# Linear attention with one routed expert on one core: tile 0's k evicted in one piece, tile 3's root on GpSimd, G of tile 0 after q unit 1

## The chip, the core and the metric

The kernel runs on one core of a Trainium2 chip. The metric is the device time of one execution in microseconds; the number to compare is the median of several. The core's engines each follow an instruction list of their own, in order, and wait for each other by semaphores: TensorE (PE in the profile), VectorE (DVE), ScalarE (ACT), GpSimd (POOL), and SyncE (SP), which here only issues DMAs.

## What is computed

One block over 2048 tokens of width 640, in bf16. With `xn` the layer norm of `x`, the output is `x + xn`, plus linear attention on `xn`, plus a small gated network that is applied to the 8 tokens with the largest router value and added to those rows.

```python
def _A_ref(x, wqkv, wo):                 # called with xn
    q, k, v = qkv[0], qkv[1], qkv[2]     # 32 heads of 20
    phi = lambda t: jnp.where(t > 0, t + 1, jnp.exp(t)) + 1e-6
    pq, pk = phi(q), phi(k)
    kv = jnp.einsum("bhsd,bhse->bhde", pk, v)
    z = jnp.einsum("bhsd->bhd", pk)
    num = jnp.einsum("bhqd,bhde->bhqe", pq, kv)
    den = jnp.einsum("bhqd,bhd->bhq", pq, z)[..., None] + 1e-6
    o = num / den
    return (lambda x, *d: x.transpose(*d))(o, 0, 2, 1, 3).reshape(B, S, D) @ wo
...
xn = _layernorm(x, axis=-1)
return x + _A_ref(xn, A_wqkv, A_wo) + _B_ref(xn, B_w_r, B_w_gate, B_w_up, B_w_down)
```

`_B_ref` (the routed network) returns its input `xn` with the 8 updated rows, which is where the `xn` in the sum comes from.

## The kernel before

The 2048 tokens are 16 tiles of 128 rows. The kernel sets the order of the instructions by hand: what the program emits first for an engine, that engine runs first. The places in the code of the functions named here are printed below.

For a tile t the first stage does this:

- `stat(t, 0)` and `stat(t, 1)` on VectorE (L176, L178): the mean and variance of the 640 columns, in two halves and an aggregate, into `mv`.
- The root: one over the square root of the variance, into `rs`. `root_act` does it on ScalarE as exp(-0.5 ln(v + eps)) in two instructions (L182, L183); `root_pool` does it on GpSimd as an addition and a power (L187, L188). Before the change tiles 0 to 3 and 8 are done by ScalarE, the others by GpSimd.
- `norm_dve(t)` on VectorE (L197) writes the normalized tile `xn`.
- The tile is transposed into `xnT`, columns on the partitions. For tiles 0 to 3 TensorE does it (`tr_pe`, L216) into PSUM banks 7 and 6, and `tr_ev` copies three of the five blocks out on ScalarE (L222) and two on VectorE (L227). For tiles 4 to 15 it is a transposing DMA that SP issues (`tr_dma`, L230).
- `k_half(t, 0)` and `k_half(t, 1)` (L238): k of the tile by TensorE, 320 columns each, from the stationary tile of `xnT`. The halves go to PSUM banks 2 and 3 for tile 1, 4 and 5 for tile 2, and 0 and 1 for the others.
- `k_act(t)` on ScalarE (L255, L256): an exp and a relu from PSUM for each half, into `ek` and `rk`, and for tiles from 1 on a copy of the router's column (L258). `k_phi(t)` on VectorE (L262) joins them into `pk`, the feature map of k.
- `g1(t)` (L269): five matmuls that add the tile's share of G = xn^T pk (first 512 columns) into banks 2 to 6.

Between these, `q_mm(u)` (L277) computes one of 20 units of q, 128 columns by 512 tokens, transposed, into bank 7 (unit 1 into bank 0); `q_act` (L286, L287) and `q_phi` (L293) apply the feature map as for k.

`const_sel8` (L368 to L375) builds a small constant mask on GpSimd, a memset and four selections; it is first used long after, in the routed network.

SP's list in this stretch: the loads of x up to tile 9 and of the q weights, then `tr_dma(4)`, `tr_dma(5)`, `tr_dma(6)`, `load_x(10, 16)` (one load of the last six tiles, 960 KB, L99), `tr_dma(7)`, and then a transpose and a weight load in turn.

From `for t in range(5, T)` (L483) on, a loop runs the same steps for the later tiles, with the normalization four tiles ahead of k. Then come the attention's small matrix products, the routed network, the remaining units of q, and the output tiles (L833 and after).

The change touches the order of calls between L410 and L460.

Of the kernel before, what the change touches and what calls it, by code (L numbers as in the profile page):

```python
# [38 lines left out]
def kernel(  # L39
# [26 lines left out]
    def sb(name, shape, dtype=BF16):  # L66
        return sm.tile(shape, dtype, tag=name, name=name)
# [30 lines left out]
    def load_x(a, b):  # L98
        SP.dma_start(x_sb[:, a:b, :], x_v[:, a:b, :])  # L99
# [52 lines left out]
    def router_col():  # L152
        PE.transpose(psb[:, 6, 512 : 512 + KC], wr5[:], ident[0:KC, 0:KC])
        A.copy(wk[:, :, D], psb[:, 6, 512 : 512 + KC])

    def router_0():
        for kc in range(KC):
            PE.matmul(
                ps[:, 6, 400:401], lhsT=xnT[:, kc, 0:P], rhs=wk[:, kc, D : D + 1],
                start=(kc == 0), stop=(kc == KC - 1),  # L160
            )
# [13 lines left out]
    def stat(t, b):  # L175
        V.bn_stats(out=stats[:, t, b, :], in_=x_sb[:, t, b * HW : (b + 1) * HW])  # L176
        if b:
            V.bn_aggr(out=mv[:, t, :], in_=stats[:, t, :, :])  # L178

    def root_act(t):  # L180
        sl = slice(t, t + 1)
        A.activation(lg[:, sl], mv[:, t, 1:2], AF.Ln, bias=eps5[:])  # L182
        A.activation(rs[:, sl], lg[:, sl], AF.Exp, scale=-0.5)  # L183

    def root_pool(t, n=1):
        sl = slice(t, t + n)
        G.tensor_scalar_add(t2[:, sl], mv[:, sl, 1], EPS_BF16)  # L187
        G.tensor_tensor(out=rs[:, sl], in0=t2[:, sl], in1=mhalf[:, 0:n], op=ALU.pow)  # L188
# [7 lines left out]
    def norm_dve(t):  # L196
        V.tensor_scalar(  # L197
            out=xn[:, t, :], in0=x_sb[:, t, :], scalar1=mv[:, t, 0:1], scalar2=rs[:, t : t + 1],
            op0=ALU.subtract, op1=ALU.mult,
        )  # L200
# [19 lines left out]
    def tr_ev(t, other=A):  # L220
        dst = xnT[:, :, t * P : (t + 1) * P]
        A.copy(dst[:, 0:3, :], psb[:, 7, 0 : 3 * P].rearrange("p (k f) -> p k f", k=3))  # L222
        src = psb[:, 6, 0 : 2 * P].rearrange("p (k f) -> p k f", k=2)
        if other is A:
            A.copy(dst[:, 3:, :], src)
        else:
            V.tensor_copy(dst[:, 3:, :], src)  # L227

    def tr_dma(t):
        nc.sync.dma_start_transpose(xnT[:, :, t * P : (t + 1) * P], xn[:, t, :])  # L230
# [3 lines left out]
    def k_half(t, b):  # L234
        b0 = K_BANK.get(t, 0)
        n = HW + (b if t else 0)
        for kc in range(KC):
            PE.matmul(  # L238
                ps[:, b0 + b, 0:n],
                lhsT=xnT[:, kc, t * P : (t + 1) * P],  # L240
                rhs=wk[:, kc, b * HW : b * HW + n],
                start=(kc == 0), stop=(kc == KC - 1),
            )
# [3 lines left out]
    def k_act(t, halves=(0, 1)):  # L247
        b0 = K_BANK.get(t, 0)
        if t not in kev:
            e = evk.tile([P, 2, HW], BF16, tag="ek", name=f"ek{t}")  # L250
            r = evk.tile([P, 2, HW], BF16, tag="rk", name=f"rk{t}")
            kev[t] = e, r
        e, r = kev[t]
        for b in halves:
            A.activation(e[:, b, :], ps[:, b0 + b, 0:HW], AF.Exp)  # L255
            A.activation(r[:, b, :], ps[:, b0 + b, 0:HW], AF.Relu)  # L256
            if b and t:
                A.copy(r_all[:, t : t + 1], ps[:, b0 + 1, HW : HW + 1])  # L258
# [8 lines left out]
    def g1(t):  # L267
        for c in range(5):
            PE.matmul(  # L269
                ps[:, 2 + c, :], lhsT=xn[:, t, c * P : (c + 1) * P], rhs=pk[:, t, 0:512],  # L270
                start=(t == 0), stop=(t == T - 1),
            )

    def q_mm(u, bank=7):
        tb, m = u // KC, u % KC
        for kc in range(KC):
            PE.matmul(  # L277
                ps[:, bank, :], lhsT=wq[:, kc, m * P : (m + 1) * P],
                rhs=xnT[:, kc, tb * 512 : (tb + 1) * 512],
                start=(kc == 0), stop=(kc == KC - 1),  # L280
            )

    def q_act(u, bank=7):
        e = evq.tile([P, 512], BF16, tag="eq", name=f"eq{u}")
        r = evq.tile([P, 512], BF16, tag="rq", name=f"rq{u}")
        A.activation(e[:], ps[:, bank, :], AF.Exp)  # L286
        A.activation(r[:], ps[:, bank, :], AF.Relu)  # L287
        kev["q", u] = e, r
# [79 lines left out]
    def const_sel8():  # L368
        cst["sel8"] = sb("sel8", [P, C], F32)
        G.memset(cst["sel8"][:], 0.0)  # L370
        for j in range(4):
            G.affine_select(
                out=cst["sel8"][:], in_=cst["sel8"][:], compare_op=ALU.not_equal, fill=1.0,
                base=-32 * j, pattern=[[-1, C]], channel_multiplier=1,
            )  # L375
# [9 lines left out]
    def stats2(t):  # L385
        stat(t, 0)
        stat(t, 1)
# [22 lines left out]
    tr_ev(1, V)  # L410
    root_act(2)
    router_col()
    k_act(0, (0,))
    stat(3, 0)
    norm_dve(2)
    stat(3, 1)
    const_sel8()
    k_half(1, 0)
    tr_pe(2)
    k_half(1, 1)  # L420
    tr_ev(2, V)
    root_act(3)
    k_act(0, (1,))
    router_0()
    k_act(1)
    stat(4, 0)
# [21 lines left out]
    norm_dve(5)  # L448
    tr_dma(5)
    q_act(0)  # L450
    g1(0)
    q_mm(1, 0)
    q_act(1, 0)
    k_phi(1)
    norm_dve(6)
    tr_dma(6)
    load_x(10, 16)
    stats2(7)
    root_pool(7)
    k_phi(2)  # L460
# [475 lines left out]
```

## Time and profile before

| | |
|---|---|
| median of 3 runs | 111.95 us (111.92 to 112.37) |
| the profiled execution | 112.4 us |
| its span, first to last instruction | 110.7 us |
| TensorE, matmuls | busy 105.0 us, 95% |
| VectorE | busy 83.2 us, 75% |
| ScalarE | busy 62.0 us, 56% |
| GpSimd | busy 41.0 us, 37% |
| granted TensorE clock | 1.0 in every slice |

In the rows below, a timeline row has the start in us, the length in us, the engine, the line of the kernel, the operation, the tile it writes and those it reads, the shapes and the count of instructions merged into the row; in brackets stands how long the engine was idle ahead of it and what ended that. Lengths of neighbouring instructions of one engine overlap a little, since an instruction begins while the one before it drains. A row of the chain of waits has the start, the length and what the end of the program was waiting for at that time. A row of the stretch table has the stretch, its length, and for matmuls, weight loads, VectorE, ScalarE and GpSimd the busy time with the count in brackets, then the granted clock, the busy share of the DMA engines and GB/s. SPq is SP issuing a DMA; the row of a DMA queue has packets, MB, and the share of 16 engines' time in the window.

### The profile page before, as it was taken

What the parts mean: (1) busy time and instruction counts of PE and PEld (TensorE: products, weight loads), DVE (VectorE), ACT (ScalarE), POOL (GpSimd) and SP (SyncE); (2) the same over time, 40 slices, a digit from 0 to 9 for tenths busy, and PEclk for the clock granted to TensorE, in tenths of its full rate; (3) what the DMA queues carried; (4) which work ended last, traced back from release to release, by engine and by line L of the source; (5) the groups of instructions that cost most, each with busy time, mean ns of one, the idle gap of its engine ahead of it and who ended that gap; (6) DMA issues with size and microseconds to landing.
All of it is one profiled execution on the core that took longest, in us unless ns stands there. A gap on an engine that the chain in (4) does not pass through costs nothing.

```text
span 110.7 us, 2559 instructions
## 1 busy us (share of the span) xinstructions
PE 105.0 (95%) x926; PEld 61.4 (55%) x926; DVE 83.2 (75%) x186; ACT 62.0 (56%) x160; POOL 41.0 (37%) x88
## 2 busy tenths in 40 slices
PE   5989799999999999999999999999999999999990
PEld 2256454665555565554436879534447766666660
DVE  1789987877999998753919964698599664788880
ACT  1449996799776666665019445588985735000000
POOL 6930273120067755899999430000000410000310
PEclk9999999999999999999999999999999999999999
DMA  3999237791758799989999979729928195783333
GB/s 84 325 341 331 103 65 63 131 328 20 197 138 160 194 182 220 199 189 287 259 248 401 391 260 266 219 68 319 356 79 177 32 330 188 169 322 118 114 121 118
DMA packets 28551, 22.46 MB, mean 203 GB/s; under 512 B 11634, under 2 KB 27258, under 8 KB 28538
## 3 DMA queue, kind: packets, MB, share of 16 engines
q1 hardware_dynamic: 23664, 18.44, 60.8%
q10 hardware_dynamic: 4810, 3.85, 11.1%
q8 instruction: 7, 0.11, 0.5%
q14 instruction: 6, 0.05, 0.2%
q0 software_dynamic: 64, 0.01, 0.1%
HBM read 14.79 MB, written 5.43 MB: 183 GB/s over the span
## 4 chain that ended last, share of the span: by engine, by line
PE 54%; DVE 22%; DMA 11%; POOL 5%; ACT 3%; issue 2%; SPq 0%; POOLq 0%; ACTq 0%
PE ps L833 19%; PE ps L277 12%; DMA x_sb<-in_A_x_dram 8%; DVE pk L262 6%; DVE stats L176 5%; DVE xn L197 5%; PE ps L269 5%; PE ps L531 4%; DVE pqT L293 3%; DMA xnT<-xn 3%; PE ps L238 3%; POOL rs L188 2%; DVE mv L178 2%; PE ps L685 2%; PE ps L768 2%
## 5 line engine op out<-in xcount | busy, mean ns | idle before, releaser
L238 PE MATMUL ps<-wk,xnT 128*128 128x320 bf16 (+1 forms) x160 | 25.0, 300 | 1.1 <-ACT xnT L222 1.0
L277 PE MATMUL ps<-xnT,wq 128*128 128x512 bf16 x100 | 23.7, 379 | 0.0
L833 PE MATMUL ps<-late,pqT 128*128 128x320 bf16 x150 | 21.8, 300 | 0.1
L238 PEld LDWEIGHTS <-xnT 128*128 128x128 bf16 x160 | 15.1, 97 | 9.7 <-ACT xnT L222 1.6
L269 PE MATMUL ps<-pk,xn 128*128 128x512 bf16 x80 | 19.6, 379 | 0.0
L255 ACT ACTIVATE ek<-ps 128x320 bf16<-128x320 f32 x32 | 14.6, 457 | 8.4 <-PE ps L238 8.4
L833 PEld LDWEIGHTS <-pqT 128*128 128x128 bf16 x150 | 13.9, 98 | 7.2 <-DVE pqT L640 1.9
L176 DVE BATCH_NORM_STATS2 stats<-x_sb 128x6 f32<-128x320 bf16 x32 | 14.7, 474 | 3.3 <-DMA x_sb<-in_A_x_dram 3.3
L286 ACT ACTIVATE eq<-ps 128x512 bf16<-128x512 f32 x20 | 12.0, 598 | 8.9 <-PE ps L277 8.9
L293 DVE SCALAR_TENSOR_TENSOR pqT<-eq,rq 128x512 bf16<-128x512 bf16 x20 | 14.2, 710 | 3.3 <-ACT rq L287 3.1
L842 DVE TENSOR_TENSOR o<-ps,x_sb 128x640 bf16<-128x640 f32 x15 | 12.4, 824 | 5.4 <-PE ps L833 3.0
L262 DVE SCALAR_TENSOR_TENSOR pk<-ek,rk 128x640 bf16<-128x640 bf16 x16 | 13.1, 823 | 3.2 <-ACT rk L256 3.2
L277 PEld LDWEIGHTS <-wq 128*128 128x128 bf16 x100 | 9.4, 98 | 10.6 <-issue 0.7
L256 ACT ACTIVATE rk<-ps 128x320 bf16<-128x320 f32 x32 | 14.6, 457 | 0.0
L208 POOL TENSOR_SCALAR x_sb<-x_sb,rs,nm 128x640 bf16<-128x640 bf16 x13 | 13.9, 1079 | 0.6
L269 PEld LDWEIGHTS <-xn 128*128 128x128 bf16 x80 | 7.6, 98 | 8.1
L287 ACT ACTIVATE rq<-ps 128x512 bf16<-128x512 f32 x20 | 11.9, 593 | 0.0
L187 POOL TENSOR_SCALAR t<-mv 128x1 bf16<-128x1 f32 x11 | 3.6, 326 | 22.2 <-DVE mv L178 22.0
L197 DVE TENSOR_SCALAR xn<-x_sb,mv,rs 128x640 bf16<-128x640 bf16 x16 | 8.3, 516 | 3.1 <-POOL rs L188 2.4
L188 POOL TENSOR_TENSOR rs<-t,mhalf 128x1 f32<-128x1 bf16 x11 | 9.4, 858 | 0.9
L884 POOL DMA_INDIRECT s_dram<-y,idx_i x1 | 1.6, 1594 | 20.4 <-ACT y L880 20.4
L869 ACT CAST o<-ps 128x160 bf16<-128x160 f32 x1 | 0.3, 293 | 13.9 <-PE ps L859 13.9
(129 smaller groups left out, 104.2 us busy)
## 6 DMA issues: line engine op xcount, KB each, us to landing
wg<-in_B_w_gate_dram SPq DMA_DIRECT2D x5, 384.0 KB, 3.4
wu<-in_B_w_up_dram SPq DMA_DIRECT2D x5, 384.0 KB, 8.9
wd<-in_B_w_down_dram SPq DMA_DIRECT2D x4, 480.0 KB, 11.0
spare<-rd SPq DMA_DIRECT2D x3, 640.0 KB, 5.5
rd<-rden ACTq DMA_DIRECT2D x1, 1280.0 KB, 7.1
out_dram<-o SPq DMA_DIRECT2D x8, 160.0 KB, 2.3
out_dram<-o ACTq DMA_DIRECT2D x7, 160.0 KB, 2.6
wo<-in_A_wo_dram SPq DMA_DIRECT2D x2, 500.0 KB, 8.2
```

Source lines behind the costliest of these rows:

```text
L176: V.bn_stats(out=stats[:, t, b, :], in_=x_sb[:, t, b * HW : (b + 1) * HW])
L197: V.tensor_scalar(out=xn[:, t, :], in0=x_sb[:, t, :], scalar1=mv[:, t, 0:1], scalar2=rs[:, t : t + 1], op0=ALU.subtract, op1=ALU.mult,)
L208: G.tensor_scalar(out=x_sb[:, t, :], in0=x_sb[:, t, :], scalar1=rs1[:, sl], scalar2=nm[:, sl], op0=ALU.mult, op1=ALU.add,)
L238: PE.matmul(ps[:, b0 + b, 0:n], lhsT=xnT[:, kc, t * P : (t + 1) * P], rhs=wk[:, kc, b * HW : b * HW + n], start=(kc == 0), stop=(kc == KC ...
L255: A.activation(e[:, b, :], ps[:, b0 + b, 0:HW], AF.Exp)
L256: A.activation(r[:, b, :], ps[:, b0 + b, 0:HW], AF.Relu)
L262: V.scalar_tensor_tensor(out=pk[:, t, :].rearrange("p (b f) -> p b f", b=2), in0=e[:], scalar=1.0, in1=r[:], op0=ALU.min, op1=ALU.add,)
L269: PE.matmul(ps[:, 2 + c, :], lhsT=xn[:, t, c * P : (c + 1) * P], rhs=pk[:, t, 0:512], start=(t == 0), stop=(t == T - 1),)
L277: PE.matmul(ps[:, bank, :], lhsT=wq[:, kc, m * P : (m + 1) * P], rhs=xnT[:, kc, tb * 512 : (tb + 1) * 512], start=(kc == 0), stop=(kc == K ...
L293: V.scalar_tensor_tensor(out=pqT[:, m, tb * 512 : (tb + 1) * 512], in0=e[:], scalar=1.0, in1=r[:], op0=ALU.min, op1=ALU.add,)
L833: PE.matmul(ps[:, b0 + b, 0:HW], lhsT=pqT[:, kc, t * P : (t + 1) * P], rhs=Ms[:, kc, b * HW : (b + 1) * HW], start=(kc == 0), stop=(kc == ...
L842: V.tensor_tensor(out=o_t[:], in0=ps[:, b0 : b0 + 2, 0:HW], in1=x_sb[:, t, :].rearrange("p (b f) -> p b f", b=2), op=ALU.add,)
```

## The change

```diff
@@ -410,17 +410,16 @@
     tr_ev(1, V)
     root_act(2)
     router_col()
-    k_act(0, (0,))
+    k_act(0)
     stat(3, 0)
     norm_dve(2)
     stat(3, 1)
+    root_pool(3)
     const_sel8()
     k_half(1, 0)
     tr_pe(2)
     k_half(1, 1)
     tr_ev(2, V)
-    root_act(3)
-    k_act(0, (1,))
     router_0()
     k_act(1)
     stat(4, 0)
@@ -448,13 +447,13 @@
     norm_dve(5)
     tr_dma(5)
     q_act(0)
-    g1(0)
     q_mm(1, 0)
     q_act(1, 0)
     k_phi(1)
     norm_dve(6)
     tr_dma(6)
     load_x(10, 16)
+    g1(0)
     stats2(7)
     root_pool(7)
     k_phi(2)
```

ScalarE evicts both halves of tile 0's k ahead of its copy of tile 2's transposed blocks, where the second half came after that copy and after tile 3's root. Tile 3's root goes from ScalarE to GpSimd, where it stands ahead of `const_sel8`; after `const_sel8` comes tile 4's root, as before. On TensorE the five matmuls of `g1(0)` come after those of q unit 1 instead of ahead of them. The amount of arithmetic is the same, and the weights of the later key-value product stay 128 columns wide.

## The prediction

> **What bounds the kernel now.** I read the chain of waits first. T4 to T15 below are the transposing DMAs of tiles 4 to 15 (`tr_dma`, L230), written by SP.
>
> ```profile
> span 110.7 us, 2559 instructions
> ...
> 19.43 6.15 DMA x_sb<-in_A_x_dram
> ...
> 47.02 3.30 DMA xnT<-xn
> ...
> 50.37 1.54 PE ps L238 x10
> ```
>
> Two stretches set the end. From 19.43 to 50.33 it is load_x(10, 16), then VectorE, then T15. From 50.37 it is TensorE alone, as the stretch table and TensorE's own timeline show:
>
> ```profile
> 50.37:107.71 57.34, 57.26 (x645) 35.14 (x645) 42.15 (x86) 26.12 (x52) 15.63 (x23) 1.00 0.74 227
> ...
> 13.14 1.54 PE L238 MATMUL ps<-wk,xnT 128*128 128x320 bf16 x10 [0.78 <-ACT xnT L222]
> ...
> 50.37 1.54 PE L238 MATMUL ps<-wk,xnT 128*128 128x320 bf16 x10 [0.16 <-DMA xnT<-xn]
> ```
>
> TensorE is busy for 57.26 of the last 57.34 us. Ahead of that it waits 0.78 us for ScalarE at 13.14 (tile 3's transposed half, L222), and 0.16 us for T15 at 50.37. The two limits almost meet: a TensorE that starts its dense part sooner gains at most 0.16 us unless T15 lands sooner, and a later T15 costs its full delay. So the change is judged by when load_x(10, 16) is issued.
>
> VectorE's first wait after 18 us that matters, and SP's issues ahead of the load:
>
> ```profile
> 25.60 0.49 DVE L176 BATCH_NORM_STATS2 stats<-x_sb 128x6 f32<-128x320 bf16 x1 [1.45 <-DMA x_sb<-in_A_x_dram]
> ...
> 15.63 2.43 SPq L230 DMA_TRANSPOSE xnT<-xn  x1
> ...
> 18.15 1.23 SPq L230 DMA_TRANSPOSE xnT<-xn  x1
> 19.43 0.57 SPq L99 DMA_DIRECT2D x_sb<-in_A_x_dram  x1
> ...
> L230 SPq DMA_TRANSPOSE xnT<-xn x12: 1202/1208/2431, 13.5 to 47.0; - x12
> ```
>
> VectorE stands idle for 1.45 us until the load lands. The load's issue follows T6 by 1.28 us (18.15 to 19.43); T6 follows T5, whose issue took 2.43 us where the median of the twelve is 1.21. Had T5 taken 1.21, SP would have been free at 16.84, and T6 would have waited for its own tile instead.
>
> **The change, part by part.** First ScalarE between 9.2 and 13 us:
>
> ```profile
> 9.22 0.44 ACT L256 ACTIVATE rk<-ps 128x320 bf16<-128x320 f32 x1
> 9.78 0.48 ACT L222 COPY xnT<-ps 128x384 bf16<-128x384 bf16 x1
> 10.16 0.30 ACT L182 ACTIVATE lg<-mv,eps 128x1 f32<-128x1 f32 x1
> 10.49 0.20 ACT L183 ACTIVATE rs<-lg 128x1 f32<-128x1 f32 x1
> 10.60 0.42 ACT L255 ACTIVATE ek<-ps 128x320 bf16<-128x320 f32 x1
> ...
> 11.23 0.44 ACT L255 ACTIVATE ek<-ps 128x320 bf16<-128x320 f32 x1
> ...
> 12.54 0.55 ACT L222 COPY xnT<-ps 128x384 bf16<-128x384 bf16 x1
> ```
>
> Tile 0's second half of k (10.60 to 11.23, two instructions, 0.63 us from start to start) moves ahead of tile 2's copy and starts about 9.55, as ScalarE issues such an instruction every 0.32 us. Tile 2's copy then starts at 10.20 instead of 9.78 (0.42 later). Tile 3's root (10.16 to 10.60, 0.44) goes away, and so does the wait of about 0.2 ahead of 9.78. The copy of tile 3 can therefore start at 10.20 + 0.38 (a copy's step, 9.78 to 10.16) + 1.31 (k of tile 1, 11.23 to 12.54) = 11.89 instead of 12.54, if TensorE has transposed tile 3 by then.
>
> Next the root of tile 3 on GpSimd. Rows of the nearest one, tile 4's, with VectorE around it, and tile 6's:
>
> ```profile
> 9.75 0.21 DVE L178 BATCH_NORM_AGGREGATE mv<-stats 128x2 f32<-128x12 f32 x1
> 10.73 0.45 DVE L197 TENSOR_SCALAR xn<-x_sb,mv,rs 128x640 bf16<-128x640 bf16 x1
> 11.61 0.21 DVE L178 BATCH_NORM_AGGREGATE mv<-stats 128x2 f32<-128x12 f32 x1
> ...
> 12.33 0.81 DVE L262 SCALAR_TENSOR_TENSOR pk<-ek,rk 128x640 bf16<-128x640 bf16 x1
> 13.05 0.44 DVE L197 TENSOR_SCALAR xn<-x_sb,mv,rs 128x640 bf16<-128x640 bf16 x1
> 15.15 0.45 DVE L197 TENSOR_SCALAR xn<-x_sb,mv,rs 128x640 bf16<-128x640 bf16 x1
> 15.52 0.82 DVE L262 SCALAR_TENSOR_TENSOR pk<-ek,rk 128x640 bf16<-128x640 bf16 x1
> 16.80 0.45 DVE L197 TENSOR_SCALAR xn<-x_sb,mv,rs 128x640 bf16<-128x640 bf16 x1 [0.46 <-POOL rs L188]
> ...
> ...
> 5.92 0.97 POOL L372 TENSOR_SCALAR_AFFINE_SELECT sel<-sel 128x8 f32<-128x8 f32 x4
> 11.91 0.25 POOL L187 TENSOR_SCALAR t<-mv 128x1 bf16<-128x1 f32 x1 [5.02 <-DVE mv L178]
> 12.25 0.58 POOL L188 TENSOR_TENSOR rs<-t,mhalf 128x1 f32<-128x1 bf16 x1
> 15.22 0.42 POOL L187 TENSOR_SCALAR t<-mv 128x1 bf16<-128x1 f32 x1
> 15.72 1.04 POOL L188 TENSOR_TENSOR rs<-t,mhalf 128x1 f32<-128x1 bf16 x1
> ```
>
> An undisturbed root on GpSimd is 0.09 (11.82 to 11.91) + 0.34 (11.91 to 12.25) + 0.58 + 0.04 to the reader (16.76 to 16.80) = 1.05 us after the variance. Tile 3's variance stands at 9.96, so its normalization starts at 11.01 instead of 10.73: VectorE is 0.28 later, with nothing behind it to hide that, because it runs without a wait from 10.73 to 15.15 (none of its rows there, below, has one in brackets). TensorE's part:
>
> ```profile
> 10.51 0.84 PE L238 MATMUL ps<-wk,xnT 128*128 128x320 bf16 x5
> 11.23 0.45 PE L216 MATMUL ps<-ident,xn 128*128 128x128 bf16 x5
> ```
>
> Tile 3's transposes follow its normalization and go from 11.23 to 11.51. Tile 2's copy, 0.48 long, now ends at 10.26 and its matmuls start at 10.51; it will end at 10.68, so they start about 10.73. They give way to the transposes after 0.72 (10.51 to 11.23), at 11.45: the 0.42 of the copy is hidden behind the 0.28. With the 0.28 undone it would cost TensorE 0.22 there. The transposes end by 11.96, so tile 3's copy starts between 11.89 and 11.98, and TensorE's dense part 0.60 after it (12.54 to 13.14 now), about 12.5: 0.6 earlier.
>
> The four selections of `const_sel8` (0.97 us and a memset, about 1.15 together) were done at 6.89. Now they are queued behind tile 3's root, which ends at 10.97, and ahead of tile 4's, which wants to start at 11.91 + 0.28 = 12.19. Without disturbance they are done at 12.1 and cost nothing. But the first meets tile 3's normalization on VectorE. The row at 15.22 is such a meeting: the same form as at 11.91 took 0.42 instead of 0.25, ending as the normalization of 15.15 ends. So the selections cost between 0 and 0.2; I take 0.2, and they end near 12.3. Tile 4's root then starts at 12.26 and its power at about 12.60.
>
> That matters because of the k of tile 0 on VectorE (12.33), which moves to 12.61. At present the power starts at 12.25, 0.08 ahead of it, and takes 0.58. At 15.72 it starts 0.20 behind one and takes 1.04, ending 0.42 after that instruction. So with the power at 12.60 against 12.61 the bounds are 0 (it slips in, as now) and this: it ends at 13.42 + 0.42 = 13.84, and tile 4's normalization starts at 13.88 instead of 13.05 + 0.28 = 13.33, a further 0.55. I take 0.55, since the start of an instruction is not yet its read, and the 0.08 of lead is nearly gone. VectorE is then 0.83 later in all.
>
> [...]
>
> Now SP. In the 1.7 us in which T5's issue dragged, the table of DMA queues has
>
> ```profile
> q8 instruction: 1, 0.02, 5.2%
> ```
>
> One packet of code, busy for 5.2% of 16 engines in the window 16.0 to 17.7, that is 0.052 x 16 x 1.7 = 1.4 us on one DMA engine. I take it that this packet stalled T5, that it follows TensorE's program, and that it moves 0.6 earlier with TensorE; T5 then takes 1.21. Bounds: 1.21 (median) and 2.43 (as now). With 0.83: T5 issues at 15.63 + 0.83 = 16.46, ending 17.67; tile 6's normalization is at 16.80 + 0.83 = 17.63, ending 18.08. T6 goes 0.03 after it (as 15.60 to 15.63 now), at 18.11, and the load at 18.11 + 1.28 = 19.39 against 19.43. VectorE, 0.83 late but with 1.45 of idle time, is ready. The load lands 0.04 sooner.
>
> [...]
>
> Last, g1(0) and q unit 1 trade places, five matmuls each:
>
> ```profile
> 15.60 1.24 PE L269 MATMUL ps<-pk,xn 128*128 128x512 bf16 x5
> 16.68 2.32 PE L277 MATMUL ps<-xnT,wq 128*128 128x512 bf16 x10
> ...
> 14.61 0.60 ACT L256 ACTIVATE rk<-ps 128x320 bf16<-128x320 f32 x1
> ```
>
> The same ten matmuls fill the same 2.16 us. Unit 1 needs bank 0, which ScalarE's read frees at 15.21, or about 14.6 after the change, and wants to start at 15.60 - 0.6 = 15.0. So 0; without ScalarE's lead it would wait 0.2 us (15.21 against 15.0), TensorE's alone. On VectorE, SP and GpSimd nothing of this edit moves; tr_dma(6) and load_x(10, 16) keep their places.
>
> **Sum.** The dense part of TensorE could start 0.6 sooner; T15 comes 0.04 sooner and decides. The profiled execution took 112.4 us for its span of 110.7; it becomes 112.36. The median of the runs is 0.45 below that execution, so 111.95 - 0.04 = 111.91.
>
> **Rivals.**
> 1. Faster: the power of tile 4 still slips in (+0.28 only) and T5 loses its stall. T5 is done at 17.12, tile 6's normalization at 17.53, T6 at 17.56, the load at 18.84: 0.59 sooner, and TensorE's 0.6 just keeps up with it. 111.36. For it: the same order of starts as now. Against: the selections in GpSimd's queue.
> 2. Slower: VectorE's 0.83 and T5's full stall. Place: the issue of T5 at 16.46, to 18.89; T6 at 18.98, the load at 20.26, 0.83 late, 112.78. It decides as soon as SP is free later than 18.15, so from a T5 that takes over 1.7 us. For it: what stalled T5 is only inferred. Against: the median transpose takes 1.21.
> 3. TensorE's gain is hidden and the load a little late: the power slips in, the stall stays. T5 from 15.91 to 18.34, T6 18.43, the load at 19.71: 0.28 late, 112.23.
>
> **How the numbers follow.** I give the forecast 0.34, rival 1 0.28, rival 2 0.20, rival 3 0.16, and 0.02 to none of these. Predicted: 111.9; its own range is 111.7 to 112.1, from half a stall more and a power that is only partly caught. The whole range, 111.2 to 112.8, takes in all four, with 0.16 us around rival 1 for the scatter of the cases. A measurement here can tell about 0.5% (0.56 us) from no change. Rival 1 stands at 0.53%, just past that: 0.18 of its 0.28 and the stray 0.02 give faster 0.20. Rival 2, with 0.06 from the upper tails of rival 3 and the forecast, gives slower 0.26. The rest, 0.54, is the same.
>
> **What would show it.** Tile 3's normalization about 0.28 later; TensorE's dense part from about 12.5, with less than 0.2 of wait where 0.78 was; tile 4's power about 1.2 us long, ending after tile 0's k (0.58 long: rivals 1 and 3); T5's issue 1.2 long (2.4: rivals 2 and 3); the load's issue within 0.15 of 19.43; and more than 0.16 us of wait for transposing DMAs late in the k loop, up to about 0.8 in all, since TensorE arrives early. I am wrong if the load's issue moves by over 0.3, or if the end moves by much else than the load does.

## The result and the profile after

The changed kernel takes 111.46 us (median of 11 runs, 111.06 to 111.77) against 112.03 us (median of 11, 111.92 to 112.52) for the kernel before on the same chips: a ratio of 0.9941 with a 95% interval of 0.9926 to 0.9957. That is 0.66 us less by the ratio and 0.57 by the medians, the place of rival 1 (111.36), not of the forecast (111.91). Here and below, a ratio leaves out runs more than 1.5% above the fastest of their kernel: three of e8, one of e11, and one of e12 that took 602.7 us.

The profiled execution after took 111.21 us for a span of 109.5. Both profiled executions lie off their medians, before by 0.34 above and after by 0.25 below, so the two traces differ by twice as much (1.19 us of span) as the kernels do.

First the two engines of tile 3's root and tile 0's k, in the timeline after (columns as before):

```profile
8.64 0.45 DVE L197 TENSOR_SCALAR xn<-x_sb,mv,rs 128x640 bf16<-128x640 bf16 x1
10.77 0.47 DVE L197 TENSOR_SCALAR xn<-x_sb,mv,rs 128x640 bf16<-128x640 bf16 x1 [0.35 <-POOL rs L188]
12.40 0.81 DVE L262 SCALAR_TENSOR_TENSOR pk<-ek,rk 128x640 bf16<-128x640 bf16 x1
...
10.16 0.58 POOL L188 TENSOR_TENSOR rs<-t,mhalf 128x1 f32<-128x1 bf16 x1
10.70 0.10 POOL L370 MEMSET sel<- 128x8 f32 x1
10.87 0.97 POOL L372 TENSOR_SCALAR_AFFINE_SELECT sel<-sel 128x8 f32<-128x8 f32 x4
11.97 0.23 POOL L187 TENSOR_SCALAR t<-mv 128x1 bf16<-128x1 f32 x1
12.29 0.57 POOL L188 TENSOR_TENSOR rs<-t,mhalf 128x1 f32<-128x1 bf16 x1
```

In this execution everything up to tile 2's normalization came 0.23 us sooner (8.64 against 8.87). Tile 3's follows 2.13 us after tile 2's, where it was 1.86: 0.27 later. The four selections took 0.97, as at their old place, though the first ran beside the normalization of 10.77. So tile 4's power started 0.11 ahead of tile 0's k, and took 0.57.

Then TensorE. Its dense part is the stretch from tile 3's k on, in which it hardly waits. The row at 16.90 is q unit 2, which was the second half of the row at 16.68 before:

```profile
11.59 2.23 PE L238 MATMUL ps<-wk,xnT 128*128 128x321 bf16 x15
...
16.90 1.24 PE L277 MATMUL ps<-xnT,wq 128*128 128x512 bf16 x5
17.98 0.71 PE L238 MATMUL ps<-wk,xnT 128*128 128x321 bf16 x4
...
48.11 1.24 PE L269 MATMUL ps<-pk,xn 128*128 128x512 bf16 x5
49.19 1.53 PE L238 MATMUL ps<-wk,xnT 128*128 128x320 bf16 x10
```

The second half of tile 2's k and tile 3's k now run in one row without the wait of 0.78, and tile 15's k at 49.19 has no wait for its transpose. Tile 4's k starts at 17.98 instead of 18.84; less the 0.23 of the start that is 0.63 sooner.

SP and VectorE:

```profile
15.68 1.64 SPq L230 DMA_TRANSPOSE xnT<-xn  x1
17.42 1.23 SPq L230 DMA_TRANSPOSE xnT<-xn  x1
18.70 0.58 SPq L99 DMA_DIRECT2D x_sb<-in_A_x_dram  x1
...
24.24 0.49 DVE L176 BATCH_NORM_STATS2 stats<-x_sb 128x6 f32<-128x320 bf16 x1
...
45.66 1.21 SPq L230 DMA_TRANSPOSE xnT<-xn  x1
```

The rows are T5, T6, the load, VectorE's first statistics on the loaded rows, and T15. T5's issue took 1.64 instead of 2.43, the load went out 0.73 sooner, and VectorE does not wait for it in this execution. T15 is issued 1.36 sooner (45.66 against 47.02).

The difference of the spans, 1.19 us, is then made of 0.23 (the start), 0.63 (TensorE's dense part) and 0.32 (tile 15's k, which could have started at 50.05 before, when the matmuls of 48.97 were issued at 0.216 each, as five from 15.60 to 16.68 were, and started at 50.37). Of these the experiments below tie only the 0.63 to the change. The start differs between executions of one kernel (tile 2's normalization at 8.87 in e2's profile and 8.72 in e6's, which are the same kernel), and e1's profile, with the front of the kernel before, has no wait ahead of tile 15's k.

### The profile page after: what moved, and what is told of

Read it like the earlier page. It is cut to its first block, busy times and chain, and to the rows that moved or that the text cites. A ratio compares the mean times of both kernels' runs of the same rounds, so it can differ in the third digit from the quotient of the medians.

```text
span 109.5 us, 2550 instructions
## 1 busy us (share of the span) xinstructions
PE 104.4 (95%) x917; PEld 61.6 (56%) x926; DVE 83.6 (76%) x186; ACT 61.4 (56%) x158; POOL 41.2 (38%) x90
## 4 chain that ended last, share of the span: by engine, by line
PE 94%; ACT 2%; issue 1%; DVE 0%
PE ps L277 20%; PE ps L832 20%; PE ps L238 19%; PE ps L269 16%; PE ps L530 4%; PE ps L147 4%; PE ps L684 2%; PE ps L767 2%; PE ps L667 1%; PE ps L858 1%; PE ps L216 1%; PE ps L598 1%; PE ps L696 1%; PE ps L777 1%; ACT rk L256 1%
## 5 line engine op out<-in xcount | busy, mean ns | idle before, releaser
L277 PE MATMUL ps<-xnT,wq 128*128 128x512 bf16 x93 | 22.9, 379 | 0.6 <-issue 0.3
L841 DVE TENSOR_TENSOR o<-ps,x_sb 128x640 bf16<-128x640 f32 x15 | 12.3, 823 | 5.4 <-PE ps L832 3.0
L262 DVE SCALAR_TENSOR_TENSOR pk<-ek,rk 128x640 bf16<-128x640 bf16 x16 | 14.3, 894 | 2.7 <-ACT rk L256 2.7
L208 POOL TENSOR_SCALAR x_sb<-x_sb,rs,nm 128x640 bf16<-128x640 bf16 x13 | 12.6, 982 | 0.6
L188 POOL TENSOR_TENSOR rs<-t,mhalf 128x1 f32<-128x1 bf16 x12 | 10.0, 834 | 1.0
```

The lines of the kernel that those rows point to most:

```text
L208: G.tensor_scalar(out=x_sb[:, t, :], in0=x_sb[:, t, :], scalar1=rs1[:, sl], scalar2=nm[:, sl], op0=ALU.mult, op1=ALU.add,)
L262: V.scalar_tensor_tensor(out=pk[:, t, :].rearrange("p (b f) -> p b f", b=2), in0=e[:], scalar=1.0, in1=r[:], op0=ALU.min, op1=ALU.add,)
L277: PE.matmul(ps[:, bank, :], lhsT=wq[:, kc, m * P : (m + 1) * P], rhs=xnT[:, kc, tb * 512 : (tb + 1) * 512], start=(kc == 0), stop=(kc == K ...
L841: V.tensor_tensor(out=o_t[:], in0=ps[:, b0 : b0 + 2, 0:HW], in1=x_sb[:, t, :].rearrange("p (b f) -> p b f", b=2), op=ALU.add,)
```

## The experiments

Two theories stand against each other. One: TensorE's dense part sets the end in most executions, and the change starts it sooner. The other, the prediction's: the issue of the load sets it, by way of tile 15's transpose.

**Which edit carries it.** The two edits alone, and the first one's two halves alone (lines between the edited ones are left out).

```diff
e1: second edit alone            e2: first edit alone
-    g1(0)                       -    k_act(0, (0,))
     q_mm(1, 0)                  +    k_act(0)
     ...                         +    root_pool(3)
     load_x(10, 16)              -    root_act(3)
+    g1(0)                       -    k_act(0, (1,))

e3: root alone                   e4: eviction alone
+    root_pool(3)                -    k_act(0, (0,))
-    root_act(3)                 +    k_act(0)
                                 -    k_act(0, (1,))
```

> The kernel before with the second edit alone: q unit 1 ahead of G of tile 0, and g1(0) after the load. Theory (the front edits carry the gain by starting TensorE's dense part sooner): no change, ratio 0.998 to 1.002; TensorE still waits about 0.8 us for tile 3's copy near 13 us, and the load of the last six tiles is issued where it was. Rival (the swap of g1(0) and q unit 1 carries the gain, since ScalarE gets unit 1 about 1.1 us sooner): ratio about 0.994.

Measured: ratio 0.9999 (0.999 to 1.0008). The swap alone does nothing. Its profile, of 112.06 us, is the better picture of a usual execution of the order before:

```profile
13.13 1.13 PE L238 MATMUL ps<-wk,xnT 128*128 128x320 bf16 x7 [0.78 <-ACT xnT L222]
...
46.46 1.21 SPq L230 DMA_TRANSPOSE xnT<-xn  x1
...
48.96 1.24 PE L269 MATMUL ps<-pk,xn 128*128 128x512 bf16 x5
50.04 1.25 PE L238 MATMUL ps<-wk,xnT 128*128 128x320 bf16 x8
```

The wait at 13 us is as before, but tile 15's transpose, issued at 46.46 and landed 3.2 later at 49.6, is ready ahead of 50.04, where tile 15's k starts without a wait. The profiled execution of before had it land at 50.33, and TensorE 0.32 late; that is nearly all of its 0.34 us over the median. So TensorE decides in this execution, whose time is that of the median before. No second execution of the kernel before itself was profiled, but e4 and e9 below agree.

> The changed kernel with g1(0) put back ahead of q unit 1: only tile 0's k in one piece and tile 3's root on GpSimd. Theory: the whole gain, ratio 0.992 to 0.996, TensorE's dense part from about 12.4. Rival (the swap carries it): ratio about 1.0.

Measured: 0.9966 (0.9953 to 0.9979, 5 runs). The first edit alone gains most or all; its dense part begins at about 12.5 (a row of 15 matmuls from 11.82, no wait in it), against 13.14.

> The kernel before with only tile 3's root moved to GpSimd; tile 0's k stays in two pieces. Theory: ScalarE loses 0.44 us ahead of tile 3's copy, but the wait of about 0.2 ahead of tile 2's copy stays; tile 3's normalization is 0.28 later; TensorE's dense part starts 0.4 sooner, ratio 0.995 to 0.998. Rival (only both edits together help, as the one piece of k is what moves tile 3's copy): ratio 0.999 or more.

Measured: 0.9979 (0.9963 to 0.9994). The dense part began 0.4 sooner, as the theory had it (12.74), and about half of that, 0.24 by the ratio, reached the end. In its profile tile 15's transpose is late again: the five matmuls of 48.57 are issued by 49.65, and tile 15's k starts at 49.92, 0.27 later.

> The kernel before with only tile 0's k in one piece; tile 3's root stays on ScalarE, after tile 2's copy. Theory: the root comes 0.4 us later, so tile 3's normalization does (about 11.1 instead of 10.7), and tile 3's copy is only 0.2 sooner: TensorE gains at most 0.2, VectorE loses 0.4; ratio 0.998 to 1.003. Rival: ratio 0.997 or less, if the eviction order is what counts.

Measured: 0.9987 (0.9978 to 0.9995), in the range of the theory. Tile 3's normalization came at 11.08, and the dense part began at 12.84, 0.3 sooner and not at most 0.2. Its profiled execution took 112.10, 0.26 over the median of its runs (111.84), and again tile 15's transpose is late by about as much:

```profile
48.70 1.24 PE L269 MATMUL ps<-pk,xn 128*128 128x512 bf16 x5
50.07 1.13 PE L238 MATMUL ps<-wk,xnT 128*128 128x320 bf16 x7
```

The five matmuls are issued by 49.78, and tile 15's k starts 0.29 after that. So the transpose did decide in the profiled executions of before, e3 and e4. In before and e4 its lateness is about what the execution lies above its median.

**The change again, beside its first edit.**

> The changed kernel itself, on the same chip as the three runs beside it. Theory (in most executions TensorE's dense part, not tile 15's transpose, sets the end, before and after): the ratio of the kernel with the front edits alone, beside it, within 0.001 of this one, both 0.993 to 0.997. Rival (the swap of g1(0) and q unit 1 adds a gain of its own once TensorE is ahead): this one lower by 0.002 or more.

> The front edits alone, g1(0) ahead of q unit 1 as before the change. Theory: as the changed kernel beside it, within 0.001. Rival (the swap has a gain of its own): 0.002 to 0.003 above it.

Measured: 0.9953 (0.9939 to 0.9967) for the change, 0.9962 (0.9947 to 0.9976) for its first edit. The two agree within their intervals. The first comparison had put them 0.0025 apart (0.9941 and 0.9966). Whether the swap adds something of the order of 0.001 stays open.

**TensorE held back.** If its sooner start is the gain, useless work of the same length must take it away.

```diff
+    warm(3, 0)
     k_half(3, 0)
     k_half(3, 1)
```

> The changed kernel with three more 512-column matmuls on TensorE ahead of tile 3's k, into bank 0, which that k overwrites: 0.65 us of work that gives nothing, so that the dense part starts as late as before the change while ScalarE, VectorE, GpSimd and SP keep the changed order. Theory (the sooner start of TensorE's dense part is the whole gain): the gain is gone, ratio 0.999 to 1.002. Rival (the gain comes from the load and tile 15's transpose, with T5's shorter issue): the load is still issued by 19, and the ratio stays at 0.994 to 0.996.

Measured: 1.0005 (0.999 to 1.002). TensorE in this kernel (one of the three useless matmuls has no record):

```profile
12.72 0.59 PE L147 MATMUL ps<-zw 128*128 128x512 bf16 x2
13.15 0.30 PE L238 MATMUL ps<-wk,xnT 128*128 128x320 bf16 x1
```

The dense part starts at 13.15, as before the change, and the whole gain is gone, with the new order on every other engine. One expectation was missed: T5's issue was 2.27 long here and the load went out at 19.55, not by 19. But tile 15's transpose landed at 49.27, 0.8 ahead of its use at 50.05, so it was not what took the gain away. This is also a second execution, of 112.09 us, in which a dense part from 13.15 without a wait for T15 gives the median of the kernel before.

**The power that is caught.** This is the case that the forecast was built on.

```diff
     root_pool(3)
     const_sel8()
+    for _ in range(2):
+        G.affine_select(
+            out=cst["sel8"][:], in_=cst["sel8"][:], compare_op=ALU.not_equal, fill=1.0,
+            base=0, pattern=[[-1, C]], channel_multiplier=1,
+        )
```

> The changed kernel with two more selections on GpSimd between tile 3's root and tile 4's, which leave the mask as it is: tile 4's power then starts about 12.8, behind tile 0's k on VectorE, and should take about 1.0 to 1.2 us. Theory (TensorE sets the end, tile 15's transpose has about 0.6 us in hand): VectorE 0.5 later up to tile 6, the load 0.4 later than in the changed kernel, tile 15's transpose lands just in time; ratio at most 0.002 above the changed kernel's. Rival (the load's issue sets the end, as the prediction had it): the 0.4 us reaches the end, 0.004 above the changed kernel's.

Measured: 1.0023 (1.0011 to 1.0034), not at most 0.002 above the changed kernel but 0.007 above it. Rows of its GpSimd and VectorE in the timeline:

```profile
12.87 0.99 POOL L188 TENSOR_TENSOR rs<-t,mhalf 128x1 f32<-128x1 bf16 x1
...
12.63 0.81 DVE L262 SCALAR_TENSOR_TENSOR pk<-ek,rk 128x640 bf16<-128x640 bf16 x1
13.90 0.45 DVE L197 TENSOR_SCALAR xn<-x_sb,mv,rs 128x640 bf16<-128x640 bf16 x1 [0.47 <-POOL rs L188]
```

And its chain of waits (start, length, what the end was waiting for):

```profile
12.87 1.01 POOL rs L188
13.90 0.45 DVE xn L197
14.38 4.30 DMA xnT<-xn
18.68 0.05 issue
18.72 1.54 PE ps L238 x10
```

Started 0.24 behind tile 0's k, the power ends 0.42 after it, and tile 4's normalization comes 2.90 after tile 3's (11.00) instead of 2.35 (10.77 to 13.12): the 0.55 that the prediction priced. It reaches TensorE first by a way that neither theory had. Tile 4's own transpose, T4, takes 4.30 us from issue to landing, where it took 2.7 before the change, and TensorE waits 0.35 us for it at 18.72. In the changed kernel T4 also takes 4.3 and lands at 17.9, just ahead of tile 4's k at 17.98. Before the change it had 2.6 us in hand; its longer flight has taken 1.7 of them and TensorE's sooner start 0.86.

The way that the prediction had is there too, behind it. The load went out at 19.44, T15 landed at 49.96, and tile 15's k starts at 50.01:

```profile
48.87 1.24 PE L269 MATMUL ps<-pk,xn 128*128 128x512 bf16 x5
50.01 1.54 PE L238 MATMUL ps<-wk,xnT 128*128 128x320 bf16 x10
```

In e2, whose execution began at the same time (tile 2's normalization at 8.87), tile 15's k starts at 49.42. So a TensorE that had T4 in time would still have been held to about 50.0 by T15, and this run does not part the two theories: either limit alone costs 0.5 to 0.6 us. The median, 112.33, lies 0.29 above the profiled execution, and what took that is not shown.

**The packet of code.** The prediction took it that a packet of code (16,384 bytes in the DMA records) stalls T5's issue and moves with TensorE.

```diff
-    warm(NWARM + 3, 0)
+    warm(NWARM + 2, 0)
+    for _ in range(10):
+        PE.matmul(ps[:, 0, 0:1], lhsT=zw[:, 0:P], rhs=zw[:, 0:1], start=True, stop=True)
```

> The kernel before with ten one-column matmuls (20 instructions of TensorE) in place of one of the nine warming ones, so that every later instruction of TensorE stands 20 places further down its program. Theory (the code packet is TensorE's and stalls T5's issue until 0.4 us after its own end): the packet comes 0.5 to 1.5 us earlier than 16.25, T5's issue takes less than 1.6 us, the load is issued by 18.8, and no wait for tile 15's transpose is left; the median moves little (0.997 to 1.001), since TensorE decides in most executions. Rival (the packet has nothing to do with TensorE's program): it starts at 16.2 as before and T5 takes 2.0 to 2.4.

Measured: 1.0043 (1.0011 to 1.0074), its runs in two groups, 111.92 to 112.18 and 113.07 to 113.71. The expected 0.997 to 1.001 was missed. The time tells nothing of the packet, because in the profile, which belongs to the slower group, TensorE took 1.52 and 1.38 us for the two halves of tile 0's k, where it took 0.85 and 0.84 before (last section), and the load went out at 19.74, not by 18.8. The issues do tell something:

```profile
14.71 2.33 SPq L232 DMA_TRANSPOSE xnT<-xn  x1
```

This is T4; T5's issue after it took 1.21, as the theory had it. The packet came at 15.49, 0.77 sooner than before although TensorE's dense part was 1.20 later, and now stalled T4. The table has for all traces, from the DMA records, the packet and the end of the issue that was stalled:

| kernel | dense part from | packet, start + length | stalled issue, end | end after packet's end |
|---|---|---|---|---|
| before | 13.14 | 16.26 + 1.41 | T5, 18.06 | 0.39 |
| e1 | 13.13 | 16.25 + 0.99 | T5, 17.68 | 0.44 |
| e3 | 12.74 | 16.22 + 1.49 | T5, 18.14 | 0.43 |
| e4 | 12.84 | 16.25 + 1.44 | T5, 18.15 | 0.46 |
| after | 12.3 | 15.88 + 1.00 | T5, 17.32 | 0.44 |
| e5 (the same) | 12.3 | 15.84 + 1.00 | T5, 17.27 | 0.43 |
| e2 | 12.5 | 16.07 + 1.00 | T5, 17.52 | 0.45 |
| e6 (the same) | 12.4 | 16.18 + 1.00 | T5, 17.58 | 0.40 |
| e8 | 14.34 | 15.49 + 1.12 | T4, 17.04 | 0.43 |
| e9 | 13.15 | 16.38 + 1.37 | T5, 18.18 | 0.43 |
| e12 | 12.2 | 16.24 + 0.99 | the load, 17.61 | 0.38 |
| e7 | 12.5 | 15.73 + 1.27 | T5, 18.07 | 1.07 |
| e10 | 12.2 | 16.24 + 1.37 | T6, 18.62 | 1.01 |
| e11 | 12.2 | 16.25 + 1.28 | T6, 18.60 | 1.07 |

In eleven of the fourteen the stalled issue ends 0.38 to 0.46 us after the packet, so it looks as if the packet's end releases it. In the last three the issue that ran long began after the packet did, and ended 1.0 to 1.1 us behind it. What sets the packet's start is not TensorE's dense part: with that anywhere from 12.2 to 13.15 the packet came at 16.2 to 16.4 in nine of the fourteen. It came sooner in e8, with 18 more instructions on TensorE (18 matmuls and 18 weight loads in the first 5 us against 9 and 9), but also in e7 with none. What it follows stays open.

**A sooner dense part still.** Three versions that keep tile 3's root on ScalarE and take work from in front of its copy. `k_part(0, 1, 0)` and `k_part(0, 1, 1)` are new calls, the exp and the relu of tile 0's second half of k.

```diff
e10, on ScalarE:                          on VectorE and SP:
     root_act(3)                               stat(5, 0)
-    k_act(0, (1,))                       +    stat(5, 1)
     router_0()                           +    root_pool(5)
-    k_act(1)                             -    k_phi(0)
+    k_act(1, (0,))                            norm_dve(4)
+    k_part(0, 1, 0)                           tr_dma(4)
     ...                                  -    stat(5, 1)
     tr_ev(3, V)                          -    root_pool(5)
+    k_part(0, 1, 1)                      +    k_phi(0)
+    k_act(1, (1,))
     k_act(2)

e11, beside that:                         e12, beside that:
-    k_act(3)                             +    load_x(10, 16)
+    k_act(3, (0,))                            norm_dve(6)
     q_mm(0)                                   tr_dma(6)
     ...                                  -    load_x(10, 16)
     q_act(0)
+    k_act(3, (1,))
```

> A version meant to start TensorE's dense part sooner than either kernel: from the kernel before, with tile 3's root left on ScalarE, and on ScalarE the relu of tile 0's second half and the second half of tile 1's k put behind tile 3's copy; on VectorE both statistics of tile 5 and tile 4's normalization come ahead of tile 0's k. Theory: tile 3's copy starts at about 11.6 as soon as its transposes are done, the dense part at about 12.2 (13.14 before, 12.4 to 12.5 after the change), and as TensorE sets the end the ratio is 0.990 to 0.994. Rival (from here on tile 15's transpose decides, as its landing cannot follow): 0.995 to 0.998, with waits for transposing DMAs late in the k loop.

Measured: 0.9947 (0.993 to 0.9963), as the change itself and between the two ranges. The dense part did start at about 12.2, and in its profile TensorE does not wait for tile 15's transpose. But ScalarE, with its work put off, reads q unit 0 late (its second read starts at 16.16 and takes 0.81, to 16.97), and the row of q units 1 and 2 stretches from 2.32 to 2.53:

```profile
15.73 2.53 PE L281 MATMUL ps<-xnT,wq 128*128 128x512 bf16 x10
18.09 0.57 PE L238 MATMUL ps<-wk,xnT 128*128 128x321 bf16 x3
```

> The deferred version with one more move on ScalarE: q unit 0 ahead of the second half of tile 3's k. In the deferred version TensorE started its dense part at about 12.2 and then lost 0.2 us ahead of q unit 2, which waits for ScalarE to read unit 0 out of bank 7. Theory (TensorE sets the end): those 0.2 us come back, tile 4's k starts at about 17.9 instead of 18.1, ratio 0.992 to 0.993. Rival (tile 15's transpose now decides): ratio as in the deferred version, 0.994 to 0.995, with a wait for it ahead of tile 15's k.

Measured: 0.9945 (0.992 to 0.997), runs from 110.95 to 112.78. The 0.2 came back: that row is 2.32 again and tile 4's k starts at 17.76, in an execution that began 0.13 sooner. The median did not follow. In its profile TensorE meets tile 15's transpose, issued at 45.95 and landed at 49.01:

```profile
47.89 1.24 PE L273 MATMUL ps<-pk,xn 128*128 128x512 bf16 x5
49.06 1.13 PE L238 MATMUL ps<-wk,xnT 128*128 128x320 bf16 x7
```

Five matmuls from 47.89 are issued by 48.97, and tile 15's k starts 0.09 later. So the two limits meet in this execution; in slower ones of this kernel, which were not profiled, the transpose may be later still. No version clearly beat the changed kernel.

> The same, with the load of the last six tiles ahead of tile 6's normalization and transpose on SP's list, so that it is issued right after T5, at about 16.7 to 17.2 instead of 18.7. Theory: VectorE no longer waits for the load near 24, tile 15's transpose lands up to 0.5 sooner, which gives the end nothing where TensorE decides: ratio within 0.001 of the version beside it, and lower only if that one waits for tile 15. Rival (tile 6's transpose now queues behind the load): it lands after 22.7, TensorE waits for it ahead of tile 6's k, and the ratio is 0.002 or more above the version beside it.

Measured: 1.0052 (1.0024 to 1.008). The rival holds. The load went out at 16.73, and tile 6's transpose, issued behind it at 17.71, took long to land (T6 took 3.5 before), as the view of L230 in a window around that issue has it:

```profile
DMA to landing us min/median/max: 6.3/6.3/6.3
```

TensorE's timeline of the same kernel:

```profile
24.08 1.54 PE L238 MATMUL ps<-wk,xnT 128*128 128x320 bf16 x10 [1.14 <-ACT rq L291]
```

The wait of 1.14 us ahead of tile 6's k is put down to ScalarE by the row; the transpose landed at 24.04, 0.04 ahead of the matmuls, and is what ended it. VectorE had its load in time and tile 15's transpose landed at 48.50, 1.9 ahead of its use: of no help, since TensorE was late.

## Why the prediction was right or wrong

The measured time lies in the stated range, and by its size what happened is rival 1 (chance 0.28), for a partly different reason. That the range held is owed to its width, which takes in four cases, and says little for the mechanism. The forecast's own range, 111.7 to 112.1, does not hold 111.46, and its own sign of being wrong, a load that moves by over 0.3, came: the load's issue moved by 0.73, or 0.50 without the sooner start. The chance of 0.54 for no clear change goes with the forecast: the first comparison lies just past the 0.5% that it could tell (0.59%), the second just short of it (0.47%).

- *Tile 3's normalization 0.28 later, its copy 0.65 and the dense part 0.6 sooner*: right; 0.27, and 0.63 for both.
- *The four selections cost 0.2*: wrong, the first of the two steps that failed and the one that mattered for the number. They cost nothing. The row that they were priced by, a root's addition that met a normalization and took 0.42, did not carry over to selections on 8 columns: they took 0.97 for four beside the normalization, the same as without it.
- *Tile 4's power is caught*: therefore wrong; it led by 0.11 and took 0.57. That a start is not yet a read, the prediction's reason to take 0.55, no run shows. What follows from it was worked out well: where e7 makes it start late, tile 4's normalization, T5, T6 and the load start at 13.90, 16.47, 18.16 and 19.44, and the forecast had 13.88, 16.46, 18.11 and 19.39. The gain is gone in e7, so this step alone is enough to part the forecast from the result.
- *T5's stall goes because the packet of code moves with TensorE*: half right. An issue does run on until 0.4 us after the packet in eleven of the fourteen traces; but the packet does not move with the dense part. T5's issue became 1.64, not 1.21, with a packet that was also shorter (1.00 against 1.41). In the three other profiles of the first edit, alone or with the swap (e2, e5, e6), it took 1.60 to 1.82 with packets of 1.00, and in e9, with a packet of 1.37, the stall was there again (2.27).
- *T15 comes 0.04 sooner and decides*: wrong, the second step that failed. The sum held the end to tile 15's transpose because the one profiled execution did, at 50.37. That execution was 0.45 over the median of the three runs then at hand, 0.34 over that of the eleven, and the prediction carried this difference along as a constant. It was nearly all the lateness of that very transpose: 0.32 us, counted from the issue of the matmuls ahead, where the row's bracket and the prediction have 0.16. In the profiles of e1 and e9, with the dense part at the old place, TensorE sets the end without waiting for T15, and the times, 112.06 and 112.09, are about the median before. So its 0.63 goes to the end in about full: 0.66 and 0.53 by the two ratios. e9 shows it from the other side.
- *The path from the load over VectorE to T15*: right. In thirteen of the fourteen traces T15 is issued 21.41 or 21.42 us after VectorE's first statistics on the loaded rows (25.60 to 47.02 before, 24.24 to 45.66 after); in e12 the load is in time. What the sum had as fixed and the traces do not is the load's own time from issue to landing: 6.15 us before, 5.52 after, and from 5.35 (e9) to 6.39 (e8) in all.
- *The swap of g1(0) and q unit 1 costs nothing*: right (0.9999 alone).
- *Rival 2's slower case* did not come, but e7 shows how near a loss lies: two more small selections on GpSimd turn the gain into a loss of 0.2%, with T4 and T15 both some 0.5 us late for TensorE.

## What to carry to other kernels

Before a sum is made against a profiled execution, ask where that execution lies among the runs: if it is slow, the wait that decides in it may be the reason, and the usual run has another limit. Where two limits meet within some tenths of a microsecond, price the change against both. And where an order depends on one instruction starting a tenth of a microsecond ahead of another, as tile 4's power does here, test it with a little more work in front of it.

## What the runs showed of the hardware that was not expected

A DMA issue on SP ran long beside a packet of code (16,384 bytes, 0.99 to 1.49 us long in the table above): T5's took 2.43 us before, where the median of the twelve is 1.21. It ended 0.38 to 0.46 us after the packet in eleven of fourteen traces. T4, which has 672 DMA packets, landed 2.7 us after its issue in the eight traces whose DMA records have them all ahead of the 16,384 bytes of code. It landed after 4.3 to 4.5 us in the five (after, e2, e5, e6, e7) in which two or more of them came only behind it. That the code delays T4 is an inference; no run moved the packet alone.

In e8, with eight warming matmuls and ten of one column instead of nine warming ones ahead of the first transposes, the profile has tile 0's k slower:

```profile
6.66 1.52 PE L240 MATMUL ps<-wk,xnT 128*128 128x320 bf16 x5
```

against 0.85 for the same five before (the first of them at 6.64). The second half took 1.38 against 0.84 (from 8.50 and 7.84); the five matmuls after that, at 9.92, took 0.85 again. The granted clock stands at 1.00 from 5 to 11 us in both kernels. Seven of its twelve runs, the profiled one (113.29) among them, were over 113 us and five at 111.92 to 112.18. What slowed these ten matmuls, and why the runs fall into two groups, is not shown.
